# Loading a constant table in six row blocks instead of three, in a fused recurrence and Fourier kernel

## The chip, the cores and the metric

The kernel runs on one core of a Trainium2 chip. A core has TensorE (PE in the profile; its weight loads are PEld), VectorE (DVE), ScalarE (ACT), GpSimd (POOL) and SyncE (SP), each with its own instruction queue, and 16 DMA engines that carry out the transfers which those queues issue. The metric is the device time of one execution in microseconds. Three runs of the kernel before gave 529.64, 529.90 and 531.75 us; the median is 529.9 us.

## The reference

First a gated linear recurrence over 4 batches, 8 heads, 768 tokens and 48 channels a head:

```python
f = 1.0 / (1.0 + np.exp(-f_logit))
for t in range(S):
    state = f[:, :, t, :, None] * state + np.einsum('bhd,bhe->bhde', k[:, :, t], v[:, :, t])
    y[:, :, t] = np.einsum('bhd,bhde->bhe', q[:, :, t], state)
```

Its heads are put side by side, so that x has 4 x 768 x 384 elements. Then a Fourier mixing block and a two-layer network with 1536 hidden channels:

```python
X = np.fft.fft(np.fft.fft(x, axis=1), axis=2)
u = x + np.real(X)
un = (u - mean) / np.sqrt(var + 1e-06)     # over the 384 channels
return u + np.maximum(un @ w_ch1, 0.0) @ w_ch2
```

## The kernel before

**Work and stages.** The recurrence is cut into 16 units, one for each batch and pair of heads; unit u belongs to batch u // 4. A unit holds its channels on 112 partitions (two heads of 48 rows at 0 and 64; the rows between are filled with a second copy of 16 rows) and 768 tokens along the free dimension, cut in chunks of 128. It runs exponentials and logarithms on ScalarE (L372, L373, L383 to L387), a running sum on VectorE (L379), products of q and k with the decays (L391, L392), small matmuls for the triangles of the chunks (L400, L559, L576), the states between chunks (L599, L607, L616), and a transpose back into token order (L636). The folds of the four quarter symmetries (L663 to L687, VectorE) prepare the Fourier transform of a batch, which is done by matmuls with tables of cosines and sines: `fnet` multiplies along the tokens with `tab` (L725) and along the channels with `cd` (L744, L759). The normalized tokens are transposed (L783) and go through the network in `projected`: batch 0 by plain matmuls (L865, L874), later ones by fast block products (L836, L888).

**Weights.** Each 128 x 384 block of the two weight matrices arrives as 64-bit words (`raw`, three buffers, L310) and is turned into float32 by ScalarE (L281), VectorE (L283, L284) and POOL (L285); a further block is loaded when POOL has freed one of the three buffers.

**Tables.** `tables` loads the sequence table `tab` (four SP transfers, L218 to L221, and a gather by POOL, L226) and the channel table `wave`, two tiles that are the subject here (L231 to L234). The first tile takes 97 rows of cosines; the second takes 96 rows of sines, which lie across two columns of `dim_tab`, hence in two transfers. A row has 384 float32 numbers, 1,536 bytes. `sort_tables` on POOL swaps two columns of `tab` (L240, L241), and copies the even and odd columns of `wave` into `cd` (L244 to L246), which then get two factors (L247, L252).

**The order.** Every engine executes its queue in order. What goes into the queues, in which sequence, is written out by hand in the string `ORDER`, one word for a step: a number is the next step of that unit, `L6fk` loads f and k of unit 6 and `L5qv` loads q and v of unit 5, `r` fetches a raw weight block, `C` converts one, `T` is `tables`, `S` is `sort_tables`, `D` are eight matmuls of no consequence that keep TensorE busy, `F0` is a step of the Fourier part of batch 0. Around the change it reads:

```python
"1 2 L5fk 5 D D 3 4 R 2 1 5 2 3 K3 C 4 3 L4qv 3 T D 2 L6fk 3 L5qv 5 C 4 D 2 4 4 3 3 4 S 2 3 C 5 K4 4 "
"F0 F0 4 F0 F0 r C K5 5 6 r C 4 L6qv 5 F0 r r 4 5 L7fk H0 H0 r 5 H0 C 6 C 5 P0 7 P0 P0 r 6 C L7qv 6 "
```

So after the table's transfers SP issues f and k of unit 6 (each in a part of 96 and one of 16 rows, L212 and L213), q and v of unit 5 (v in L206 and L207) and then a raw block (L310). Semaphore waits between engines and transfers are added by the framework. SP's transfers signal eight semaphores in turn, and a transfer is issued only when the one before it on its semaphore has landed.

Of the kernel before, what the change touches and what calls it, by code (L numbers as in the profile page):

```python
# [83 lines left out]
def kernel(  # L84
# [13 lines left out]
    nc = tc.nc  # L98
# [8 lines left out]
    QS, QD = S // 4, DM // 4  # L107
# [107 lines left out]
    def tables():  # L215


        nc.sync.dma_start(out=tab[:, 0, 0], in_=seq_tab[:, 0, 0])  # L218
        nc.sync.dma_start(out=tab[1:16, 0, 1], in_=seq_tab[1:16, 0, 1])
        nc.sync.dma_start(out=tab[16:128, 0, 1], in_=seq_tab[16:128, 0, 1])  # L220
        nc.sync.dma_start(out=tab[0:1, 0, 1], in_=seq_tab[64:65, 1, 1])  # L221
        back = p1.tile([128, 1], U32, tag="most", name="back")
        nc.gpsimd.iota(back, pattern=[[0, 1]], base=1, channel_multiplier=3)
        nc.gpsimd.iota(back[64:128], pattern=[[0, 1]], base=3 * C + 1, channel_multiplier=-3)
        nc.gpsimd.iota(back[64:65], pattern=[[0, 1]], base=2, channel_multiplier=0)
        nc.gpsimd.indirect_dma_start(  # L226
            out=tab[:, 1].rearrange("p t m -> p (t m)"), out_offset=None,
            in_=seq_tab.rearrange("p j t m -> (p j) (t m)"),
            in_offset=bass.IndirectOffsetOnAxis(ap=back, axis=0))

        wave = [p2.tile([128, DM], F32, tag="un", name=f"wave{i}") for i in range(2)]  # L231
        nc.sync.dma_start(out=wave[0][0:QD + 1], in_=dim_tab[0:QD + 1, 0])
        nc.sync.dma_start(out=wave[1][0:63], in_=dim_tab[65:128, 1])
        nc.sync.dma_start(out=wave[1][63:QD], in_=dim_tab[0:QD - 63, 2])  # L234
        return wave

    def sort_tables(wave):
# [712 lines left out]
    with tc.manual_schedule():  # L950
        for word in ORDER.split():
            kind, n = word[0], int("0" + "".join(c for c in word if c.isdigit()))
# [14 lines left out]
            elif kind == "B":  # L967
                weight_sum()
            elif kind == "H":
                next(behind[n], None)  # L970
            elif kind == "r":
                fetch()
            elif kind == "V":
                reread()
            elif kind == "D":
                busy()
            elif kind == "C":
                weights()
            elif kind == "c":
                sizes()  # L980
            elif kind == "R":
                fetch(3)
            elif kind == "L":
                load(n, *word.strip("L0123456789"))
            elif kind == "I":
                start()
            elif kind == "i":
                nc.sync.dma_start(out=ident, in_=ident_in)
            elif kind == "T":
                wave = tables()  # L990
            elif kind == "S":
                sort_tables(wave)
            elif kind == "Z":
                zeros()
            elif kind == "M":
                flag = judge()
# [92 lines left out]
```

## Time and profile before

| | |
|---|---|
| median of three runs | 529.9 us |
| the profiled execution | 528.67 us |
| its span, first to last instruction | 526.9 us |
| PE busy | 497.4 us (94%) |
| DVE busy | 379.6 us (72%) |
| ACT busy | 224.8 us (43%) |
| POOL busy | 58.0 us (11%) |
| mean granted TensorE clock | 0.981 |
| SP's transfers (queue 1) | 19,142 packets, 43.43 MB |

The page divides the span into 40 slices of 13.2 us and gives each engine's busy share in tenths, the TensorE clock that was granted (9 means 90% or more of full speed) and the load of the DMA engines. A later part follows the chain of work that ended last back from the last instruction, and shares the span out over it. Lines of a timeline read: start in us, duration in us, engine and source line, operation, tile written and tile read, and in brackets how long the engine was idle before and what ended that. "SPq" is SP's queue. A line of waits reads: who, for whom, us in total, how often, the longest. "Issue" is time in which an engine waited for nothing that the profile shows.

### The profile page before, as it was taken

The numbers are of one execution on the slowest core, as the hardware profiler recorded it, in microseconds if no ns is written. First come the engines' busy times: TensorE is split into PE (matmuls) and PEld (weight loads), VectorE is DVE, ScalarE is ACT, GpSimd is POOL, SyncE is SP. The second block draws the span as 40 slices with busy tenths as digits, with TensorE's granted clock in tenths as the row PEclk, the third lists the DMA queues.
The fourth block names the chain that finished last, engine by engine and source line by source line (L and its number), as shares of the span: only waits on it lengthen the run. The fifth ranks groups of instructions, "written<-read, shape, count | busy, mean of one in ns | idle before, by whom it ended". The sixth has DMA issues, their size and how long they took to land.

```text
span 526.9 us, 13784 instructions
## 1 busy us (share of the span) xinstructions
PE 497.4 (94%) x5854; PEld 456.9 (87%) x5854; DVE 379.6 (72%) x746; ACT 224.8 (43%) x529; POOL 58.0 (11%) x85
## 2 busy tenths in 40 slices
PE   4867789999999999999999999999999999999995
PEld 4756668866899889999999889999899999999995
DVE  3777998998896258696598886686787566757561
ACT  6474667655530371444634534451441405132230
POOL 3110633351001000100001000000000000010000
PEclk9788899999999999999999999999999999999998
DMA  8998635674021121103031212110323112421101
GB/s 212 258 242 214 188 106 159 193 214 124 12 76 63 39 70 44 43 1 117 23 89 51 55 55 71 47 63 14 106 61 104 47 61 91 145 66 60 34 1 36
DMA packets 20462, 48.15 MB, mean 91 GB/s; under 512 B 3366, under 2 KB 5991, under 8 KB 20391
## 3 DMA queue, kind: packets, MB, share of 16 engines
q1 hardware_dynamic: 19142, 43.43, 29.5%
q0 software_dynamic: 1104, 3.54, 1.8%
q8 instruction: 48, 0.79, 0.6%
q14 instruction: 24, 0.19, 0.1%
q10 hardware_dynamic: 144, 0.20, 0.1%
HBM read 42.44 MB, written 4.72 MB: 89 GB/s over the span
## 4 chain that ended last, share of the span: by engine, by line
PE 81%; DVE 9%; issue 1%; ACT 1%; DVEq 0%
PE ub L836 24%; PE fx L888 16%; PE fz L888 12%; PE up L865 7%; PE z L725 3%; PE po L874 3%; PE y L559 3%; PE mix L744 2%; PE pt L783 2%; PE ds L599 2%; DVE w L284 2%; PE y L616 2%; PE yt L636 1%; PE sc L400 1%; PE st L538 1%
## 5 line engine op out<-in xcount | busy, mean ns | idle before, releaser
L843 DVE TENSOR_TENSOR h<-h,ub 128x512 f32<-128x512 f32 x81 | 55.1, 686 | 40.4 <-PE ub L836 40.3
L692 POOL DMA_INDIRECT out_dram<-x,place x16 | 17.8, 1112 | 383.5 <-DVE x L918 261.6
L841 ACT ACTIVATE h<-ub 128x512 f32<-128x512 f32 x54 | 32.2, 597 | 58.6 <-PE ub L836 58.1
L865 PE MATMUL up<-unT,w 128*128 128x256 f32 x216 | 49.3, 381 | 0.6 <-ACT unT L784 0.6
L845 ACT ACTIVATE h<-h 128x512 f32<-128x512 f32 x54 | 33.9, 631 | 33.3 <-DVE h L843 33.3
L888 PE MATMUL fx<-block,h 128*128 128x192 f32 x264 | 46.6, 327 | 0.0
L836 PE MATMUL ub<-unT,w 128*128 128x128 f32 x360 | 46.6, 280 | 0.0
L865 PEld LDWEIGHTS up<-unT,w 128*128 128x128 f32 x216 | 40.2, 190 | 6.3 <-ACT unT L784 0.8
L888 PE MATMUL fx<-w,h 128*128 128x192 f32 x264 | 45.4, 327 | 0.0
L836 PEld LDWEIGHTS ub<-unT,w 128*128 128x128 f32 x360 | 43.2, 191 | 0.7
L888 PEld LDWEIGHTS fx<-block,h 128*128 128x128 f32 x264 | 43.3, 190 | 0.1
L888 PEld LDWEIGHTS fx<-w,h 128*128 128x128 f32 x264 | 42.7, 190 | 0.3 <-ACT unT L784 0.2
L836 PE MATMUL ub<-wide 128*128 128x128 f32 x288 | 39.0, 281 | 0.0
L836 PE MATMUL ub<-wide,w 128*128 128x128 f32 x288 | 38.2, 280 | 0.0
L285 POOL TENSOR_TENSOR w<-w,raw 128x384 uint32<-128x384 uint32 x24 | 27.2, 1132 | 75.9 <-DVE w L284 39.1
L836 PEld LDWEIGHTS ub<-wide 128*128 128x128 f32 x288 | 34.6, 191 | 1.0 <-issue 0.4
L836 PEld LDWEIGHTS ub<-wide,w 128*128 128x128 f32 x288 | 34.3, 191 | 1.1 <-DVE h L843 0.3
L379 DVE TENSOR_TENSOR_SCAN W<-g,bound 112x768 f32<-112x768 f32 x12 | 21.0, 1750 | 9.2 <-ACT g L373 9.2
L784 ACT COPY unT<-pt 128x384 f32<-128x384 f32 x24 | 11.6, 487 | 35.8 <-PE pt L783 35.8
L867 ACT ACTIVATE h<-up 128x256 f32<-128x256 f32 x36 | 13.5, 380 | 30.3 <-PE up L865 30.3
L559 PE MATMUL y<-at,v 64*48 64x64 f32 (+1 forms) x768 | 19.3, 229 | 6.6 <-DVE at L404 2.9
L559 PEld LDWEIGHTS y<-at,v 64*64 64x64 f32 (+1 forms) x768 | 15.6, 135 | 10.3 <-issue 4.1
(188 smaller groups left out, 1003.0 us busy)
## 6 DMA issues: line engine op xcount, KB each, us to landing
raw<-in_w_ch_dram SPq DMA_DIRECT2D x24, 384.0 KB, 6.1
v<-in_v_dram SPq DMA_DIRECT2D x16, 288.0 KB, 4.5
k<-in_w_ch_dram SPq DMA_DIRECT2D x12, 384.0 KB, 3.7
g<-in_w_ch_dram SPq DMA_DIRECT2D x12, 384.0 KB, 3.4
k<-in_qkf_dram SPq DMA_DIRECT2D x14, 288.0 KB, 4.0
g<-in_qkf_dram SPq DMA_DIRECT2D x12, 288.0 KB, 6.4
q<-in_qkf_dram SPq DMA_DIRECT2D x12, 288.0 KB
wide<-in_qkf_dram SPq DMA_DIRECT2D x10, 288.0 KB, 5.4
```

Source lines behind the costliest of these rows:

```text
L285: nc.gpsimd.tensor_tensor(bits, bits, lo, ALU.add)
L379: nc.vector.tensor_tensor_scan(W, g, bound[:R], 0.0, ALU.add, ALU.min)
L559: nc.tensor.matmul(y[FILL[g], c // 3, c % 3 * C + t.start:c % 3 * C + t.stop], lhsT=vals[rows, o:o + (64 if g == 0 else D)], rhs=weights, ...
L692: nc.gpsimd.indirect_dma_start(out=out.rearrange("b s d -> (b s) d"), out_offset=bass.IndirectOffsetOnAxis(ap=place[:, b, i:i + 1], axis=0 ...
L725: nc.tensor.matmul(z[:, cols], lhsT=src[:, j, lo:hi], rhs=tab[:, t, T % 2, cols], start=(i == 0), stop=(i == len(parts) - 1), skip_group_c ...
L836: nc.tensor.matmul(banks[bank][:, m * 128:(m + 1) * 128], lhsT=block(w)[:, m * 128:(m + 1) * 128], rhs=tokens(a), start=(new and m == 0), ...
L841: nc.scalar.activation(out, got, AF.Copy, scale=1.0 if how == "=+" else -1.0)
L843: nc.vector.tensor_tensor(out, out, got, ALU.add if how == "+" else ALU.subtract)
L845: nc.scalar.activation(out, out, AF.Relu)
L865: nc.tensor.matmul(pp[:, :256], lhsT=w1[:, kt, m * 128:(m + 1) * 128], rhs=unT[:, kt], start=(kt == 0), stop=(kt == 2))
L874: nc.tensor.matmul(po[:, :DM], lhsT=h[:, m, t], rhs=w2[:, m], start=(m == 0), stop=(m == NF - 1))
L888: nc.tensor.matmul(out, lhsT=h[:, m], rhs=blocks[i][:, m], start=(start and m == 0), stop=(m == H - 1), skip_group_check=True)
```

## The change

The rows of the two `wave` tiles are the same, from the same places in the table; they arrive in six transfers in place of three. Tile 0's 97 rows come as 96 and 1, tile 1's first 63 rows as 48 and 15, its last 33 as 32 and 1. The tuple gives the tile, the first row in it, the number of rows and where in the table they begin (QD is 96). All six are issued by SP, one after another, in the place of the three. `ORDER` and everything else stay as they are.

```diff
         wave = [p2.tile([128, DM], F32, tag="un", name=f"wave{i}") for i in range(2)]
-        nc.sync.dma_start(out=wave[0][0:QD + 1], in_=dim_tab[0:QD + 1, 0])
-        nc.sync.dma_start(out=wave[1][0:63], in_=dim_tab[65:128, 1])
-        nc.sync.dma_start(out=wave[1][63:QD], in_=dim_tab[0:QD - 63, 2])
+        for w, o, n, rows in ((0, 0, QD, dim_tab[:, 0]), (0, QD, 1, dim_tab[QD:, 0]), (1, 0, 48, dim_tab[65:, 1]),
+                              (1, 48, 15, dim_tab[113:, 1]), (1, 63, 32, dim_tab[:, 2]), (1, 95, 1, dim_tab[32:, 2])):
+            nc.sync.dma_start(out=wave[w][o:o + n], in_=rows[:n])
         return wave
```

## The prediction

> **What bounds the kernel now.** I read the page first, for the chain and the clock.
>
> ```profile
> PEclk9788899999999999999999999999999999999998
> ...
> PE 81%; DVE 9%; issue 1%; ACT 1%; DVEq 0%
> PE ub L836 24%; PE fx L888 16%; PE fz L888 12%; PE up L865 7%; PE z L725 3%; PE po L874 3%; PE y L559 3%; PE mix L744 2%; PE pt L783 2%; PE ds L599 2%; DVE w L284 2%; PE y L616 2%; PE yt L636 1%; PE sc L400 1%; PE st L538 1%
> ```
>
> TensorE sets the end; from about 122 us to the end the chain is almost gapless matmul, so a delay or gain made earlier that reaches TensorE there is carried to the end in full. No DMA is in the chain. The edited loads issue near 45 us, so next the SP queue's own timeline there, and its waits from 44 to 62 us.
>
> ```profile
> 45.04 0.23 SPq L232 DMA_DIRECT2D wave<-in_dim_tab_dram  x1
> 45.33 0.85 SPq L233 DMA_DIRECT2D wave<-in_dim_tab_dram  x1
> 46.23 0.32 SPq L234 DMA_DIRECT2D wave<-in_dim_tab_dram  x1
> ...
> 48.50 0.42 SPq L212 DMA_DIRECT2D q<-in_qkf_dram  x1
> 54.52 0.31 SPq L213 DMA_DIRECT2D q<-in_qkf_dram  x1
> 54.96 0.35 SPq L206 DMA_DIRECT2D v<-in_v_dram  x1
> ...
> 55.99 0.53 SPq L310 DMA_DIRECT2D raw<-in_w_ch_dram  x1
> ```
>
> ```profile
> SPq L213 <- DMA wave<-in_dim_tab_dram: 5.6, 1, 5.6
> SPq L310 <- POOL w L285: 3.7, 1, 3.7
> ```
>
> The queue stands 5.6 us, waiting for the 97-row load. The trace's semaphore numbers say why this instruction: SP transfers signal eight semaphores in turn, and each issue waits for the transfer eight issues back. The packet records show the transfer itself: its 1,536-byte packets run one behind another on a single ring, 65 to 130 ns each, up to 54.67. The 63-row load's eight other rings landed by 48.12, its last at 54.94; the 33-row load's at 48.32 and 55.14. Unit 6's f and k rows, issued from 46.75 to 48.03, landed on their other rings by 52.82 and on the slow ring from 55.90 to 56.96; unit 5's q at 57.84 and 58.03, its v at 58.63, the weight block of 55.99 at 61.50.
>
> Is anybody waiting for those? The chain from 30 to 75 us, and the waits of all engines from 44 to 75:
>
> ```profile
> 44.78 1.97 issue
> 46.75 0.62 PE ds L599 x12
> ...
> 52.82 0.81 PE ds L599 x16
> ...
> 53.65 0.76 DVE stt L607
> ...
> 55.22 0.96 DVE q L391
> ```
>
> ```profile
> PE y L559 <- DVE at L404: 2.4, 1, 2.4
> ...
> PE ds L599 <- issue: 2.0, 1, 2.0
> ...
> POOL pair L240 <- DMA tab<-in_seq_tab_dram,back: 1.1, 1, 1.1
> ```
>
> From 53.65 to 78.8 the chain is VectorE back to back. The only compute instruction there that waits for a DMA is POOL's L240, on the gathered half of the position table, not on the edited loads.
>
> **What the Trainium skill says.** "DMA: Bandwidth & Descriptors", Why a DMA increments its semaphore by 16 and not by 1: a transfer uses the largest number of engines up to 16 that divides its slowest dimension, starting from the lowest-numbered. That gives 97 rows one, 63 nine, 33 eleven; afterwards 96, 48 and 32 get 16, 15 gets 15, one row gets one. The trace agrees: the three loads' semaphores got 1, 9 and 11 landings, the last of each late on the one busy ring. The same page, Queues, rings and completion order: each engine consumes a queue's descriptors in ring order; this explains why every later load's last piece is late too. "SBUF — State Buffer", Who interferes with whom: a DVE operation with two SBUF inputs and a GpSimd operation that reads SBUF exclude each other for a whole instruction. The trace agrees: VectorE's L669 at 59.32 took 1.19 us, elsewhere 0.35, while POOL's L285 of 59.30 ran. "Runtime: NRT & Kernel Launch", Instruction fetch mechanics: instructions come in 16 KiB blocks of 256, by DMA. The trace has these packets, and the 1.97 us of TensorE above is such a block: asked for after 40.50, moved from 43.73 to 45.14, in use at 46.75.
>
> **The change part by part.**
>
> *The one-ring transfer goes.* The 97-row load's 8.4 us on one ring become six packets on each of 16, plus one packet. Its landing: from 45.04, at the 2.8 us that the 63-row load's other rings took, about 47.9 (estimate). The ring with 97+7+3=107 packets keeps 6+1+3+1+2+1=14, or about 0.9 us at 65 ns; a ring outside the first eleven gets 12 where it had none, 0.8 us more.
>
> *Three more issues on SP.* Each takes about 0.43 us. The first eight issues still wait for the older landings on their semaphores (45.02, 45.31, 46.19, 46.68, 47.05, 47.27, 47.66, 46.66). So the six parts go at 45.04, 45.33, 46.23, 46.70, 47.1 and 47.5, unit 6's f rows at about 47.9 and 48.3 (46.75 and 47.12 now), its k rows, which now wait for the 96-row part, at 48.7 and 49.1 (47.64 and 48.03), q of unit 5 at 49.6 and 50.0 (48.50 and 54.52), v at 50.5 and 50.9 (54.96 and 55.41). The weight block is held by POOL until 54.49: 54.5 in place of 55.99. The next block waits for POOL's L285 of 59.30 and goes at 60.33 as now. From there SP is unchanged.
>
> *What those loads are worth.* First uses, against the landings above: q of unit 5 by VectorE L391 at 69.15, 11.1 us later; the weight block by ScalarE at 72.36, 10.9 us; f of unit 6 by ScalarE L372 at 73.43, over 17 us; v of unit 5 by TensorE at 77.50, over 18 us. The edited rows are copied by POOL from 62.51, 7.4 us after landing. So 5.6 us of stall is worth nothing, 1.2 us of later issue costs nothing. Were the cover gone, the first would gain at most 5.6 us and the second cost 1.2.
>
> *POOL starts earlier.* L240 waits until 61.39 for the gather (issued 55.44, last landing 61.34), whose packets share the rings with v and the weight block. Earlier loads let it land sooner, but POOL is in L285 until 60.30. So L240 moves by 0 to 1.04 us. POOL's copies now block VectorE: L666 by 0.17, L667 by 0.17, L668 by 0.05, L669 by 0.18 us over their usual times, 0.57 together. Moved by a full microsecond, about half of them fall under L404 (60.44 to 61.43), which reads PSUM and has its usual length beside POOL; the rest block the next four sums alike. Bounds: 0.57 gained to 0.6 lost (double the blocking); I take 0.3 gained. POOL also tests three more landings, 0.04 us each by its present semaphore instructions, with 1.7 us of idle time before L285 of 69.38.
>
> *TensorE's instruction block.* The block moved from 48.68 to 49.64 is usable about 1.6 us later by the case above, at 51.25; TensorE enters it at 52.25. Spare: 1.0 us. The even spread puts at most 0.8 us more on its ring. Bounds: 0 to 2.2 us lost (the longest such stop, 32.08 to 34.25); I take 0.
>
> Sum: 0 + 0 − 0.3 + 0 = −0.3 us on a span of 526.9, so 526.6, and 528.4 for the profiled execution's own 528.67. The median of the runs, 529.9, is 1.2 above that execution; it goes to 529.6.
>
> **The rivals.** *The stall is on the path* (faster): for it speaks that it is SP's longest DMA wait here and holds five loads; against it the margins of over 10 us and a chain without DMA. Full price 5.6 us: 524.3. *The fetch comes late* (slower): more rings are busy at 48.7 us, and once that block is over 1.0 us late, TensorE stops at 52.25, on the chain, by up to 2.2 us. The clock then may fall to half for a period, as after the wait that ends at 61.48 (half from 63.1 to 66.5): TensorE's 3.95 busy us from 54 to 60 would need 7.9, up to 1.9 us over the stage. Together at most 4.1, 534.0; with half the stop and no clock loss 531.0. Against it: 0.8 us of added packets does not use up 1.0. *The change doesn't do what it says*: the one-row and 15-row parts or the eight-issue wait hold SP elsewhere. Even so the loads keep their margins: 529.9.
>
> **How the numbers follow.** My forecast, hidden loads with POOL a little earlier, 0.62; nothing gained at all, 0.18; stall on the path, 0.10; fetch late, 0.10. Half a per cent, 2.65 us, is about what a measurement of this kernel tells from no change (its three runs span 2.1). Of the path case nearly all is faster by more than that; of the fetch case 0.07 is slower by more and 0.03 not. Faster 0.10, same 0.83, slower 0.07. The likeliest case's own range is 528.3 to 531.3. To hold 8 in 10 with the outer bounds I go from 527.0 to 532.2.
>
> **What would show it.** Right: six loads, none on one ring for microseconds; SP without the 5.6 us wait, q and v of unit 5 issued near 50 us; L240 starting between 60.3 and 61.4; VectorE still back to back from 53.6 to 78.8. Wrong: a TensorE "issue" gap near 52 us with a new half-clock stretch behind it, or L391 of unit 5 starting microseconds earlier than 69.15.

## The result, and the profile after

The median went from 529.77 us (20 runs) to 531.12 us (20 runs): ratio 1.0017, with a 95% interval of 0.9997 to 1.0037. (The ratios in this document are taken over the runs; they are not quotients of the two medians, which would be 1.0025 here.) That is no change that this measurement can tell from nothing, as forecast; 531.12 lies 1.5 us above the 529.6 us predicted and within the range of 527.0 to 532.2. The profiled execution of the changed kernel took 533.93 us with a span of 531.9 us, 5.0 us more than the span before. It is the third slowest of its 20 runs, 2.8 us above their median, while the profiled execution before was 1.1 us below the median of its kernel. Most of the 5.0 us is not the change, as will be seen, and that is the trap of this case: one profile beside another seems to show a loss of 1%.

First the page of the changed kernel, its clock in 40 slices and the chain by engine and by line.

```profile
PEclk9967899999999999999999999999999999999999
...
PE 80%; DVE 9%; issue 1%; ACT 1%; DMA 1%; POOL 0%; DVEq 0%; POOLq 0%
PE ub L836 24%; PE fx L888 16%; PE fz L888 12%; PE up L865 7%; PE z L725 3%; PE y L559 3%; PE mix L744 2%; PE y L616 2%; DVE w L284 2%; PE pt L783 2%; PE po L874 2%; PE ds L599 2%; PE yt L636 2%; PE sc L400 1%; PE st L538 1%
```

The chain is nearly the same: TensorE with 80% in place of 81%, the same lines in nearly the same order. Two things differ. In the clock row the second to fourth slices were 7, 8 and 8 before; now they are 9, 6 and 7. And there is 1% of DMA. From the chain of the changed kernel, 112 to 124 us:

```profile
115.60 4.68 DMA raw<-in_w_ch_dram
```

This is a weight block that POOL's L285 releases. It is not one of the loads around the change, which had all landed more than 45 us earlier, and a second profile of the kernel before, shown below, has the like.

The next view is SP's own timeline in the changed kernel, with the columns as before: start, duration, what was issued.

```profile
44.70 3.32 SPq L234 DMA_DIRECT2D wave<-in_dim_tab_dram  x6
48.13 0.31 SPq L212 DMA_DIRECT2D wide<-in_qkf_dram  x1
...
50.73 0.81 SPq L212 DMA_DIRECT2D q<-in_qkf_dram  x1
51.58 0.42 SPq L213 DMA_DIRECT2D q<-in_qkf_dram  x1
52.05 0.42 SPq L206 DMA_DIRECT2D v<-in_v_dram  x1
...
56.87 0.35 SPq L310 DMA_DIRECT2D raw<-in_w_ch_dram  x1
```

And the queue's waits from 44 to 64 us:

```profile
SPq L310 <- POOL w L285: 6.5, 1, 6.5
SPq L310 <- POOL back L223: 3.8, 1, 3.8
SPq L234 <- DMA q<-in_qkf_dram: 1.0, 1, 1.0
```

The six parts go out in 3.32 us, the 5.6 us wait for a `wave` transfer is gone, and q's second part follows its first by 0.85 us instead of 6.0. No ring is left microseconds behind the others now: the semaphore records put the last landing of the 96 rows at 48.46, of the last single row at 49.15, of unit 5's q at 55.10 and 55.39 and of its v at 56.35. SP's only long waits are for POOL, which holds the raw blocks.

Nobody was waiting for these loads. From the chain of the changed kernel, 25 to 82 us:

```profile
46.03 1.66 issue
47.70 1.01 PE ds L599 x12
...
71.69 0.96 DVE q L391
```

L391, the first user of unit 5's q, starts at 71.69, 16.3 us after the landing; before, the lead was 11.1 us. The lead grew by 5 us and the time didn't fall. L391 itself is 2.5 us later than before (69.15). From 53.65 us on VectorE set the chain before; here TensorE and ScalarE set it until 63.56 us, TensorE at half its clock from 44.7 to 51.5.

### The profile page after: what moved, and what is told of

Read it like the earlier page. It is cut to its first block, busy times and chain, and to the rows that moved or that the text cites. A ratio compares the mean times of both kernels' runs of the same rounds, so it can differ in the third digit from the quotient of the medians.

```text
span 531.9 us, 13790 instructions
## 1 busy us (share of the span) xinstructions
PE 501.5 (94%) x5854; PEld 459.9 (86%) x5854; DVE 378.1 (71%) x746; ACT 225.1 (42%) x529; POOL 56.3 (11%) x85
## 4 chain that ended last, share of the span: by engine, by line
PE 80%; DVE 9%; issue 1%; ACT 1%; DMA 1%; POOL 0%; DVEq 0%; POOLq 0%
PE ub L836 24%; PE fx L888 16%; PE fz L888 12%; PE up L865 7%; PE z L725 3%; PE y L559 3%; PE mix L744 2%; PE y L616 2%; DVE w L284 2%; PE pt L783 2%; PE po L874 2%; PE ds L599 2%; PE yt L636 2%; PE sc L400 1%; PE st L538 1%
## 5 line engine op out<-in xcount | busy, mean ns | idle before, releaser
L285 POOL TENSOR_TENSOR w<-w,raw 128x384 uint32<-128x384 uint32 x24 | 27.3, 1139 | 81.7 <-ACT raw L281 25.3
L559 PE MATMUL y<-at,v 64*64 64x64 f32 (+1 forms) x768 | 20.2, 235 | 4.2 <-DVE at L404 2.2
L192 PE MATMUL y<-bound 128*128 128x128 bf16 x168 | 14.6, 260 | 9.6 <-POOL bound L175 4.6
```

The source lines that it names most:

```text
L192: nc.tensor.matmul(spare, lhsT=bound[:, :C], rhs=bound[:, :C], start=not started, stop=True, skip_group_check=True)
L285: nc.gpsimd.tensor_tensor(bits, bits, lo, ALU.add)
L559: nc.tensor.matmul(y[FILL[g], c // 3, c % 3 * C + t.start:c % 3 * C + t.stop], lhsT=vals[rows, o:o + (64 if g == 0 else D)], rhs=weights, ...
```

## The experiments

### How far do two profiles of one kernel differ?

The question is where 5.0 us of span came from. So the kernel before was run once more, as a kernel of its own, and the changed kernel twice more, on two chips. Nothing is edited in these three.

> The kernel before, unchanged, timed against itself: a ratio of 1.000 whose interval tells what this comparison can resolve. Both theories expect its span to differ from 526.9 us by some microseconds in either direction if the half-clock stretches of TensorE fall elsewhere; if a difference of 5 us in the span came from the change alone, this span should be within 1 us of 526.9.

> The changed kernel again, on one chip with the next two. Hidden loads: 1.000 within 0.002, like the three transfers of 112, 63 and 48 rows. If its three added issues cost something, it repeats the first ratio of 1.0017 and lies above the kernel with three transfers by 0.3%.

> The changed kernel a third time, on one chip with these two. The earlier comparisons gave 1.0017 and 1.0031; a real cost of 0.2% stays between 1.001 and 1.004 here, and the stop of 0.3 us at 412 us is in its profile again. If the earlier figures were chance, 1.000.

The kernel before against itself: 529.24 us (14 runs) against 529.38 (55 runs), ratio 0.9996 [0.9973, 1.0018]. The changed kernel: 531.19 against 530.03, 1.0031 [1.0012, 1.0049], and 530.04 against 529.21, 1.0029 [1.0008, 1.0051]. Two of these intervals, both of the changed kernel, lie above one: a loss of some 0.3% there, far under what one profile seemed to show. The profiled spans were 526.1 us for the control and 528.9 and 529.7 for the changed kernel.

The following lines are stretches of the span, with columns: the stretch, its length, busy time and number of instructions of PE, PEld, DVE, ACT and POOL, the granted TensorE clock, DMA share, GB/s. First the kernel before:

```profile
0.00:40.00 40.00, 26.51 (x581) 23.55 (x585) 24.42 (x31) 25.09 (x49) 8.87 (x33) 0.86 0.97 239
40.00:75.00 35.00, 27.87 (x652) 23.00 (x649) 30.61 (x60) 19.24 (x53) 12.81 (x20) 0.91 0.57 158
```

The same kernel, run as the control:

```profile
0.00:40.00 40.00, 25.92 (x669) 22.89 (x669) 26.57 (x37) 26.06 (x50) 8.87 (x33) 0.93 0.94 246
40.00:75.00 35.00, 29.17 (x561) 24.06 (x561) 29.90 (x58) 19.80 (x56) 12.69 (x21) 0.83 0.58 158
```

The changed kernel:

```profile
0.00:40.00 40.00, 27.66 (x573) 24.51 (x573) 22.95 (x29) 24.73 (x48) 8.84 (x33) 0.87 0.96 246
40.00:75.00 35.00, 27.61 (x577) 22.68 (x577) 28.45 (x58) 17.58 (x51) 10.33 (x19) 0.80 0.55 141
```

The two profiles of one program have a clock of 0.91 and of 0.83 in the stretch from 40 to 75 us. The clock is lowered in whole stretches, and where they fall differs from run to run: in the kernel before at 15.3, 35.8 and 63.1 us (6.8, 6.8 and 3.4 us long), in the control at 14.2, 38.1 and 58.6 (3.4, 6.8, 6.8), in the changed kernel at 27.7, 44.7 and 61.8 (10.2, 6.8, 6.8). Every length is a multiple of 3.4 us. This fits the Trainium skill ("TensorE: Matmul & The Clock Gate", What's actually happening): the throttle looks at TensorE's activity in a free-running window of about 3.4 us, so where a change of clock falls varies from run to run. The traces agree.

The control also has SP's stall, 5.5 us, and its chain, from 108 to 120 us, has the weight block that the first profile of the same kernel lacks:

```profile
111.24 4.59 DMA raw<-in_w_ch_dram
```

To see where the span differs, I lined up the matmuls of the profiles by their order. In the table, "start" is when the L599 begins that follows TensorE's stop for instructions (46.75 in the kernel before), "stage" is from there to the start of the fourth channel matmul of the Fourier part (L744), "main" from there to the start of the 14th matmul from the end, and "tail" what follows it (all us).

| profile | start | stage | main | tail | span |
|---|---|---|---|---|---|
| before | 46.75 | 28.32 | 443.19 | 8.65 | 526.9 |
| control (the same) | 43.62 | 29.73 | 443.73 | 8.99 | 526.1 |
| after | 47.70 | 29.92 | 445.23 | 9.09 | 531.9 |
| after, second | 46.46 | 28.32 | 445.00 | 9.14 | 528.9 |
| after, third | 46.37 | 30.10 | 444.26 | 8.94 | 529.7 |

So of the first profile's 5.0 us, 0.95 arose ahead of the stage, 0.76 of it before the first of the edited loads was issued, and 1.60 in the stage itself. But one program starts it at 46.75 or 43.62, and needs 28.32 or 29.73 us for it; the changed kernel has 28.32 in its second profile, to the hundredth what the kernel before has. In both kernels the stage is 28.3 us long where TensorE has its full clock in the stage's first 14 us, and 29.7 to 30.1 where a lowered stretch reaches into them. A stretch of 3.4 us that begins 16 us after the start shows no cost: a profile further below (the changed kernel shifted by one more instruction) has no lowered stretch in the stage at all, and it takes 28.3 us too. Only the column "main" is longer in all three profiles of the changed kernel, by 0.5 to 2.0 us. That is the part to explain, and its sign agrees with three ratios that all stand above one.

### How large is the cover?

If the loads are hidden by about 11 us, then two more one-ring transfers of 97 rows ought to cost nothing, and three ought to begin to show. The changed kernel issues them behind its six parts, into a tile whose blocks are written later anyway:

```diff
+        for i in range(2):
+            nc.sync.dma_start(out=w2[0:QD + 1, NF - 1 - i], in_=dim_tab[0:QD + 1, i])
         return wave
```

(`range(3)` in the second kernel; lines after it are numbered two higher.)

> The changed kernel with two more transfers of 97 rows each behind the table's six, into a part of the second weight matrix that is written later: about 16.8 us of work on the lowest ring, twice that of the kernel before, while the table itself lands early. Hidden loads: the ring is free near 66 us, q of unit 5 lands near 68 (first use 69), the weight blocks near 72 (first use 72.4): ratio 1.000 to 1.002. Stall on the path: each such transfer costs about 8 us, so 1.015 or more over the kernel before.

> The same with three such transfers, 25 us on the lowest ring. Hidden loads: the ring is free near 74 us, q of unit 5 lands near 76, 6 to 7 us after its use at 69, the weight block near 78, 5 us late: 5 to 7 us slower than the kernel before, ratio 1.010 to 1.013, with VectorE waiting for q of unit 5 or for a weight block. Stall on the path: 17 us and more, 1.030.

With two added transfers: 530.29 us against 529.38, ratio 1.0009 [0.9987, 1.0031]. The added loads landed at 58.61 and 68.05, and unit 5's q at 70.79, about 1 us before its user starts at 71.82. POOL waited 3.5 us for the gathered half of the position table, which also has packets on the slow ring; it cost nothing that can be measured. With three: 534.22 us against 529.38, 1.0080 [1.005, 1.011], a clear loss. Its waits of all engines from 44 to 85 us:

```profile
DVE q L393 <- DMA q<-in_qkf_dram: 5.7, 1, 5.7
...
ACT raw L283 <- DMA raw<-in_w_ch_dram: 4.3, 1, 4.3
```

and its chain:

```profile
64.57 10.26 DMA q<-in_qkf_dram
...
74.92 0.97 DVE q L393
```

Here a DMA stands in the chain: q's second part, issued at 64.57, landed at 74.83, and VectorE started 0.09 us later (L393 is L391 with the two added lines). That is how these loads look when they are on the path; in no profile of the kernel before or of the changed one does the chain hold the table's loads or those issued behind them up to 57 us. The cover is real and ends about where the lead of 11 us said it would: q lands 12.8 us later with two added transfers than in the kernel before (58.03), with a user that starts 2.7 us later, and 16.8 us later with three. The loss of 4.2 us (0.8% of 529.4) is below the 1.0 to 1.3% that I had expected, and below VectorE's 5.7 us of waiting.

### Which transfer stalls SP?

Only the first transfer is split, into 96 rows and 1; the 63 and the 33 rows stay whole.

```diff
-        nc.sync.dma_start(out=wave[0][0:QD + 1], in_=dim_tab[0:QD + 1, 0])
+        nc.sync.dma_start(out=wave[0][0:QD], in_=dim_tab[0:QD, 0])
+        nc.sync.dma_start(out=wave[0][QD:QD + 1], in_=dim_tab[QD:QD + 1, 0])
```

> Only the 97 rows are split, in 96 and 1; the 63 and 33 rows stay whole, on nine and eleven rings. If the 97-row transfer alone holds the ring, SP's wait of 5.6 us is gone and all table rows have landed by 49 us; if the 63 and 33 rows matter too, a wait of a microsecond or more remains. The span within 5 us of 526.9 in either case.

One run took 532.51 us, with a span of 530.6. SP has no wait for a `wave` transfer any more, q's two parts go at 49.08 and 49.45, and all of the table's rows had landed by 47.5 (the 63 rows at 47.27, the 33 at 47.47). So the stall and the late last pieces of the 63 and 33 rows came from the 97-row load alone; the other two splits add issues and free nothing that this one hadn't. With one run its time can't be ranked.

### The same benefit without more transfers

Three transfers again, with 112, 63 and 48 rows, whose counts divide well; the 15 surplus rows each in the first and last load are never read.

```diff
-        nc.sync.dma_start(out=wave[0][0:QD + 1], in_=dim_tab[0:QD + 1, 0])
+        nc.sync.dma_start(out=wave[0][0:112], in_=dim_tab[0:112, 0])
         nc.sync.dma_start(out=wave[1][0:63], in_=dim_tab[65:128, 1])
-        nc.sync.dma_start(out=wave[1][63:QD], in_=dim_tab[0:QD - 63, 2])
+        nc.sync.dma_start(out=wave[1][63:111], in_=dim_tab[0:48, 2])
```

> The channel table in three transfers of 112, 63 and 48 rows: no transfer on a single ring and no additional issue; the surplus rows are never read. Hidden loads: ratio 1.000 within 0.002, SP's 5.6 us wait gone. If the three added issues are what made the change slower by 0.17%: 1.000 here, with the changed kernel near 1.002. If the earlier traffic on all rings is what costs: 1.002 here too. If the stall were on the path: 0.990.

> The three transfers of 112, 63 and 48 rows again. Hidden loads: 1.000 within 0.002, so that the earlier 0.9985 does not repeat as a gain clear of the interval. A gain from the freed ring: 0.9985 or below again.

Against the kernel before: 528.60 us to 529.38, ratio 0.9985 [0.9967, 1.0003], and 530.25 to 530.03, 1.0015 [0.9996, 1.0035]. The SP stall is gone in this way as well (q's parts at 49.47 and 50.35, v at 50.72), with no more issues than before. The two comparisons lie on both sides of one and both intervals hold it: removing the stall is worth nothing measurable, whichever way it is done. In its first profile the stage was 28.33 us and in its second 29.81, the same two lengths once more, and only the second has a lowered stretch in the stage's first 14 us.

If the lowered clock in this stage costs 1.4 us, perhaps it can be avoided. The next kernel is the one just shown with three more of the words `D`, each eight matmuls of no consequence that keep TensorE busy, ahead of `S` in the order:

```diff
-... D 2 4 4 3 3 4 S 2 3 C 5 K4 4 "
+... D 2 4 4 3 3 4 D D D S 2 3 C 5 K4 4 "
```

> Three transfers of 112, 63 and 48 rows, and three more groups of eight matmuls of no consequence where TensorE waits for VectorE near 59 to 61 us. If the half-clock stretch that follows this wait is what spreads the stage from the stopped L599 to the first L744 between 28.3 and 29.9 us, the stretch is gone or is no longer than 3.4 us and the stage takes about 28.3 us: 0.5 to 1.5 us faster than without, ratio 0.996 to 0.999. If the clock in this stage does not matter, 1.000; if the added matmuls delay L559, 1.002.

A miss: 531.68 us to 530.03, ratio 1.0021 [0.9999, 1.0043], where I expected a gain of 0.1 to 0.4%. A lowered stretch of 6.8 us still came at 58.2 us. TensorE had stood still for 2.03 us up to 56.75, waiting for ScalarE, and the new fillers ran only from 61.29 on. The second profile of the 112-row kernel has the same stop, 2.02 us. The experiment was also aimed at the wrong stretch: by the stages above it is a lowered clock early in the stage that goes with the longer time, here from 44.5 to 47.9 us, and the fillers come well after it. Whether fillers in another place would help wasn't tried.

### What makes the main part longer?

In all three profiles of the changed kernel, and in neither of the kernel before, TensorE falls back by 0.34 to 0.36 us at one place near 412 us. It is an addition on VectorE for which TensorE waits. From VectorE's timeline, first in the kernel before (the bracket is the idle time before the instruction):

```profile
411.62 0.69 DVE L843 TENSOR_TENSOR h<-h,ub 128x512 f32<-128x512 f32 x1 [1.39 <-PE ub L836]
```

and in the changed kernel:

```profile
416.20 0.69 DVE L843 TENSOR_TENSOR h<-h,ub 128x512 f32<-128x512 f32 x1 [1.73 <-PE ub L836]
```

The record of its wait on the semaphore stands at 411.56 and 415.78; it started 0.06 us later before and 0.42 us later now. Nothing that the profile shows it to need was late. What has changed is its number: it is VectorE's 703rd instruction before and its 704th now. The trace also holds packets of 8,192 bytes that carry instructions, without naming the engine that they are for. In each of the 13 profiles of this document one of them starts within 1 us of VectorE's 448th instruction and one within 1 us of its 704th, which is 256 further on; at the 576th, halfway between, none is nearer than 4.8 us. So I read the 448th and the 704th as the ends of blocks that are fetched whole.

The shift by one comes from the change itself. With six transfers instead of three, two steps that later read or reuse the tiles have more transfers to wait for, and the framework adds semaphore instructions: two on POOL (L244) and one on VectorE (L780). VectorE has 870 instructions in place of 869.

The kernels with two and three added slow loads are a control that was not planned: they have the six parts and POOL's two added waits, but VectorE has 869 instructions there, the addition is its 703rd, and it starts without the delay (with two, 1.39 us of idle time as in the kernel before):

```profile
414.82 0.69 DVE L845 TENSOR_TENSOR h<-h,ub 128x512 f32<-128x512 f32 x1 [1.39 <-PE ub L838]
```

To test this without any change of the loads, one instruction was moved from POOL to VectorE in both kernels:

```diff
-        nc.gpsimd.memset(eps, 1e-6)
+        nc.vector.memset(eps, 1e-6)
```

> The kernel before with one VectorE instruction more in its queue (the first small fill, of eps, moved from POOL to VectorE), which shifts VectorE's instruction stream by one as the changed kernel's additional wait at L780 does. If that shift is what costs, the last L843 before the 704th VectorE instruction (at 411.6 us before) starts some 0.4 us after its wait in place of 0.06, TensorE then waits at L836 for it, and the time is 0.3 us or more above the kernel before: ratio 1.001 to 1.002. If the changed kernel's added issues and traffic cost it: no such stop, 1.000.

> The changed kernel with the same move, a shift of two. If the shift matters, the stop at the 704th VectorE instruction takes another form and the ratio differs from the changed kernel's beside it, in either direction by up to 0.001; if the added issues cost, it equals it, near 1.002.

The kernel before, shifted by one, has the delay to the hundredth: the wait's record stands at 410.95 and the addition, now the 704th, starts at 411.37.

```profile
411.37 0.69 DVE L843 TENSOR_TENSOR h<-h,ub 128x512 f32<-128x512 f32 x1 [1.74 <-PE ub L836]
```

The changed kernel shifted once more, where that addition is the 705th, starts it 0.06 us after its wait. It has lost 0.34 us elsewhere, near 285 us, where TensorE waits for VectorE's L815:

```profile
PE ub L836 <- DVE wide L815: 0.4, 1, 0.4
```

The same delay stands behind this loss, 256 instructions earlier: the 448th of VectorE is here L392, which follows a wait. First the kernel before, where it is the 446th, then this one:

```profile
279.22 0.96 DVE L392 TENSOR_TENSOR g<-W,k 112x768 f32<-112x768 f32 x1
279.11 0.96 DVE L392 TENSOR_TENSOR g<-W,k 112x768 f32<-112x768 f32 x1 [0.44 <-DVE q L391]
```

It starts 0.40 us after the end of its wait in place of 0.04, and from the start of the L391 ahead of it to the first L815 behind it VectorE takes 6.91 us in place of 6.57. In the other kernels the 448th doesn't directly follow a wait, and it starts without a delay.

The end of the kernel shows the price. From a matmul near 249 us (L599) to the 14th from the end, TensorE takes 269.3 to 269.5 us in the eight profiles without the VectorE instruction added (the kernel before and its control, the 112-row kernel twice and once with fillers, the one with only the 97 rows split, the two with added slow loads). It takes 269.7 to 269.9 us in the five that have one or two added (the changed kernel three times, and the two shifted ones).

That the delay goes with the place of the instruction in the stream, and that the added semaphore instruction moves it, is shown. That fetching the next block is what holds the last instruction of a block is an inference from the packets' times and from the distance of 256. The times of these kernels can't tell 0.07%: 529.83 to 529.21 us, 1.0014 [0.9992, 1.0037], and 529.69 to 529.21, 1.0010 [0.9990, 1.0031].

### What stays open

The three comparisons of the changed kernel give 1.0017, 1.0031 and 1.0029, 0.9 to 1.6 us. The place of the VectorE instruction explains 0.35 us of it. In two of its three profiles TensorE also lost 0.8 us within L559 of unit 12, near 248 us; but that came in one profile of the 112-row kernel, in the one with fillers and in the one with only the 97 rows split, too, and not in the third of the changed kernel. The main part of the 112-row kernel, which adds no wait, was 443.92 and 444.43 us, the latter more than the third of the changed kernel. That of the kernel with only the 97 rows split, which adds no VectorE instruction, was the longest of all, 445.37 us, and that of the changed kernel with the two added slow loads took 442.98 us, less than the kernel before. From an L783 near 123 us on, TensorE takes 123.40 or 123.41 us for the same 1,280 matmuls in all 13 profiles, up to the place near 248 us. So what is left arises ahead of 123 us, where two profiles of one program differ as well. I can't assign the remaining 0.5 to 1.3 us to any instruction, and with intervals of ±0.2% a part of it may not exist.

## Why the prediction was right, and where it was not

*The one-ring transfer goes*: right. The 96 rows landed 3.8 us after the first issue, where I estimated about 2.9; the last row of the whole table was in at 49.15.

*Three more issues on SP*: right. The six parts were forecast from 45.04 to 47.5 and went from 44.70 to 47.75; unit 6's f was forecast at 47.9 and went at 48.13; q and v of unit 5 were forecast from 49.6 to 50.9 and went from 50.73 to 52.56. The steps were a little longer than 0.43 us where a wait fell among them, which adds up to 1.7 us on the last, all within the cover. The weight block behind them was forecast at 54.5 and went at 56.87, 54.22 and 55.65 in the three profiles; in each of them SP waited for POOL, and the gain of 1.5 us over 55.99 is in one of them alone.

*What those loads are worth, nothing*: right, and shown by doses. Two slow transfers fit under the cover and three do not, and only then does one of these loads stand in the chain. That no DMA is in the chain held for the one profile that I had read; the control of the same kernel has weight blocks in its chain.

*POOL starts earlier, −0.3 us*: this step failed. Its first half happened in the profile after. In the timeline of POOL after:

```profile
62.77 1.00 POOL L285 TENSOR_TENSOR w<-w,raw 128x384 uint32<-128x384 uint32 x1 [3.80 <-ACT raw L281]
63.72 0.42 POOL L240 COPY pair<-tab 128x8 f32<-128x8 f32 x1
```

L240 stands directly behind L285, with no wait for the gather; the gather itself took 4.3 us from issue to landing in place of 5.9. But the control, with the loads of the kernel before, has this as well:

```profile
56.75 1.00 POOL L285 TENSOR_TENSOR w<-w,raw 128x384 uint32<-128x384 uint32 x1 [2.96 <-ACT raw L281]
57.70 0.52 POOL L240 COPY pair<-tab 128x8 f32<-128x8 f32 x1
```

So the wait of 1.1 us, on which the term was built, comes and goes without any change of the loads (the kernel before shifted by one instruction has it again, 1.0 us). And the gain in VectorE did not come. Over their usual durations the folds from L663 to L687 took 1.4 us more in the kernel before (this includes the one that runs beside L285), 1.4 us more in the control, and 0.9, 1.5 and 1.4 us more in the three profiles of the changed kernel; in the first of these L285 ran mostly beside L404, which it doesn't lengthen. In the others the blocking moved from some folds to others and kept its size: the term is about 0, inside its bounds, at a value that I had not taken.

*TensorE's instruction block, 0*: right. No profile has a TensorE stop for a block near 52 us. The stop at the block before it is there in the changed kernel too, the 1.66 us of "issue" ahead of 47.70; it varies by itself, and the control has none at all.

*A term that was missing*: the price of the added waits. I counted three tests on POOL at 0.04 us each and hid them under its idle time; POOL got two, of 0.02 and 0.04 us, and the third went to VectorE, of which I did not think. That one instruction of 0.05 us moved an addition that TensorE waits for onto the 704th place, and cost 0.35 us, about the size of the term that I had worked out with most care. The Trainium skill calls the crossing of a block "mostly hidden" ("Runtime: NRT & Kernel Launch", Instruction fetch mechanics); if the 704th place is such a crossing, as I infer, it is not hidden here.

The rival of a stall on the path is refuted by the doses and by the 112-row kernel, that of a late fetch by the chains. The rival that nothing is gained came closest to what was measured, if it is widened by a loss of 0.1 to 0.3%. The central number had the wrong sign: 0.3 us gained was forecast, and 0.9 to 1.6 us lost were measured. That 531.12 lies in the range is owed to the width of the range and not to these small terms; so far it was luck. Two of the signs that I had named, L240 between 60.3 and 61.4 us and VectorE back to back from 53.6 to 78.8, do not hold in the first profile (63.72, and TensorE in the chain until 62.83); they tell more of the profile than of the change.

## What to carry to other kernels

Ask of a stalled queue who uses what it carries, and when: 5.6 us of stall with 11 us of lead behind it are worth nothing, and the lead can be measured by adding slow transfers until one shows in the chain. Splitting a transfer can have a price even so, as a part can be a further semaphore to wait for at the next use of the tile, and thus an instruction more on an engine that others wait for; a row count that divides well, with surplus rows that nobody reads, spreads it over the rings without that. And before explaining a difference between two profiles, take a second one of the same kernel: here it would have shown that POOL's wait for the gather and a chain without DMA are not in every profile of the kernel before.

## What was unexpected in the hardware

VectorE's 704th instruction started 0.42 us instead of 0.06 us after its wait wherever it followed one, in four profiles of two kernels, and once the 448th, 256 places earlier, started 0.40 us instead of 0.04 us after its own. One program's profiles differ by 1.4 us in one stage of 28 us, and by 3.1 us in the 47 us before it, with the stretches of lowered TensorE clock at different places. And one transfer of 97 rows on a single ring delayed the last pieces of all the loads issued in the 3.5 us after it: with it split, the last pieces of the 63 and 33 rows came at 47.27 and 47.47 us instead of 54.94 and 55.14.
